# Gate sums of the next block moved into the loop over row tiles, and PSUM copies cut in halves, in an adaLN layer's forward and backward pass

## The chip, the cores and the metric

One core of a Trainium2 chip. The metric is device time in microseconds of one execution, and below it is the median of three runs.

## What is computed

One token (1 x 1024) goes through a layer with adaptive layer norm, attention over the last 4096 rows of a cache, and a gated feed-forward part. The program returns the output and the gradients of nine inputs. The part that the change touches is the feed-forward part, forward and backward:

```python
h = _layernorm(x) * (1 + cb) + sb
g = h @ w_gate            # 1024 x 3584
u = h @ w_up              # 1024 x 3584
out = x + gb * ((_sigmoid(g) * u) @ w_down)      # 3584 x 1024
# and, through jax.vjp, the gradients of w_gate, w_up, w_down and h
```

With one token every weight gradient is an outer product of two vectors and as large as its weight. The gradients of the two caches (1 x 4 x 65536 x 128 each) are zero outside the last 4096 rows, and these zeros have to be written too; the page shows 114 writes of 1024 KB from the tile of zeros, which fill the queue of transfers wherever the program puts them.

## The kernel before, in words

The program is written in one order by hand; each engine (PE, ACT, DVE, POOL for the software DMA queue, SP for the hardware one) carries out its share of it in that order, waiting on semaphores that the framework derives from the tiles. Transfers are issued by POOL (weights in, gradients out, zeros) and by SP (w_down and its gradient).

The feed-forward part runs over 7 blocks q of 512 hidden columns. For a block:

- `load_ug` (L863, DMA on POOL at L865) has brought w_up and w_gate, 1024 x 512 each, as eight row tiles j of 128 rows, rows 0 to 3 and rows 4 to 7 in separate DMAs of 512 KB. There are two buffers, `ug_v[:, q % 2]`; block q + 2 goes where block q was, so its loads wait until block q's gradients have been stored from there.
- `load_wd` on SP (L852) has brought 512 rows of w_down in two halves s. There is one buffer, `wd_v`.
- `front(q)` (L955) sums h2 x w_up and h2 x w_gate on PE in 64 narrow matmuls; `gates(q)` (L961, L962) takes sigmoids on ACT; `hh_ops(q)` makes small products on DVE.
- `ffn_mm(q, s)` (L973, PE) is the forward product with w_down. `wd_ttr(q, s)` (L979 through the helper at L210, DVE) is the row sums of w_down x upstream gradient. `wd_outer(q, s)` (L983 through L206, DVE) overwrites w_down's tile with its gradient, and `store_wd` (L855) sends it out.
- `dug_part(q)` makes the gradient of gate and up: eight transposes on PE into one PSUM tile of 128 x 1024 bf16 (tp_dug, L992), then one ACT copy that spreads it as a row over all partitions (`dug_b`, which lives in the tile scr, L993).
- The loop over the row tiles j (L1021): `ttr(w, w, dug_b, ...)` on DVE (L210) sums w x dug_b, then the tile is overwritten with an outer product h2[j] x dug_b, on ACT for j below 5 (`outer_act`, L241) and on DVE for the rest (`outer_dve`, L206). After j = 3 the rows 0 to 3 are stored (`store_ug`, L869 on POOL), after j = 7 the rest. `zero(z[..])` puts one or more writes of zeros into POOL's queue at four places per block.

Besides this there are 45 side jobs that no block needs but the work after the loop does: `tr_unit` (L833) transposes a 128 x 1024 block in place, eight PE transposes into a PSUM tile (tp_side, L837) and one ACT copy back (L838). `side(n)` runs the next n of them. They and `dug_part` take their PSUM tile from the same pool with one buffer (`new_tp`), so that they follow each other on it. In a block before the change they stand after the outer products of tiles 1 to 4 (in the first block 3 and 4), after `wd_ttr(q + 1, 0)`, after `gates(q + 1)` and at the end.

After the loop over j a block goes on with block q + 1: `wd_ttr(q+1, 0)`, `front`, `gates`, `hh_ops`, `ffn_mm` twice, `wd_outer(q+1, 0)`, `wd_ttr(q+1, 1)`, `dug_part(q+1)`, the loads of block q + 2, `wd_outer(q+1, 1)`.

Of the kernel before, what the change touches and what calls it, by code (L numbers as in the profile page):

```python
# [19 lines left out]
D = 1024  # L20
# [38 lines left out]
def kernel(  # L59
# [26 lines left out]
    nc = tc.nc  # L86
# [60 lines left out]
    def dep(later, earlier):  # L147
        tc.add_manual_dep(later.ins, earlier.ins.name,
                          mybir.DependencyInfo(mybir.DependencyClass.Sync, mybir.DependencyReason.DATA),
                          reason="pace")  # L150

    def zero(n, after=None):
        for _ in range(n):
            if len(zleft) <= keep[0]:
                return
            region, narrow_ = zleft.pop(0)
            first = None
            if narrow_:
                nc.gpsimd.inc_swdge_sem([], [], mode="reset_dge_cursor")  # L160
                n = nlen - ncount.pop()
                first = nc.gpsimd.dma_start(
                    out=rest[0:NS, 0:nlen * 128].rearrange("p (t x) -> p t x", t=2)[:, :, n * 64:(n + 1) * 64],
                    in_=zeros[0:NS, 0:64].rearrange("p (t x) -> p t x", t=1).broadcast_to([NS, 2, 64]))
                ins = nc.gpsimd.dma_start(
                    out=region[8:P, :].bitcast(FP32).rearrange("(t p) x -> p t x", t=2),
                    in_=zeros[0:60, :].rearrange("p (t x) -> p t x", t=1).broadcast_to([60, 2, ZW // 2]))
            else:
                ins = nc.gpsimd.dma_start(out=region.bitcast(FP32), in_=zeros[:, :])  # L169
            if after is not None:  # L170
                dep(first or ins, after)
# [5 lines left out]
    def next_pool():  # L177
        nrot[0] += 1
        return rot[nrot[0] % len(rot)]
# [8 lines left out]
    def new_tp(name="tp"):  # L188
        p, tag = next_pool()
        return p.tile([P, 1024], BF16, name=name, tag=tag)  # L190
# [4 lines left out]
    def mulv(out, a, b):  # L195
        return tt(out, a, b, ALU.mult)

    def addv(out, a, b):
        return tt(out, a, b, ALU.add)

    def cp(out, a):
        return nc.vector.tensor_copy(out=out, in_=a)  # L202
# [6 lines left out]
    def ttr(out, w, b, acc):  # L209
        return nc.vector.tensor_tensor_reduce(out=out, in0=w, in1=b, scale=1.0, scalar=0.0,  # L210
                                              op0=ALU.mult, op1=ALU.add, accum_out=acc)
# [31 lines left out]
    def outer_dve(out, col, b):  # L243
        return ts(out, b, col, ALU.mult)
# [200 lines left out]
    def side(n=1):  # L445
        for _ in range(n):
            if jobs:
                jobs.pop(0)()
# [61 lines left out]
    for tb in range(4):  # L510
        c = slice(tb * 1024, (tb + 1) * 1024)
        nc.scalar.activation(out=P_bf[:, c], in_=P_bf[:, c], func=ACT.Exp, bias=nbias[:, 0:1], scale=SCALE,
                             accum_out=ssum4[:, tb:tb + 1])
        tp = new_tp("tp_pT")
# [111 lines left out]
    for g in range(G):  # L626
        nbank = bank_pair("n_ps", g)
        for t_ in range(KT):
            s = g * KT + t_
# [200 lines left out]
    b_sec(3, 4, 40)  # L830
    zero(Z_CB)

    def tr_unit(blk, dst=None):  # L833
        def run():
            tp = new_tp("tp_side")
            for i in range(8):
                nc.tensor.transpose(tp[:, i * P:(i + 1) * P], blk[:, i * P:(i + 1) * P], ident_bf[:, :])  # L837
            nc.scalar.copy(out=blk if dst is None else dst, in_=tp[:, :])  # L838
        return run

    wg_view = B_w_gate.rearrange("(j p) n -> p j n", p=P)
# [9 lines left out]
    def load_wd(q, s):  # L851
        nc.sync.dma_start(out=wd_v[:, 2 * s:2 * s + 2, :], in_=wd_dram(B_w_down, q, s))  # L852

    def store_wd(q, s):
        nc.sync.dma_start(out=wd_dram(out_8, q, s), in_=wd_v[:, 2 * s:2 * s + 2, :])  # L855
# [7 lines left out]
    def load_ug(q, j0, n):  # L863
        for k, view in ((0, wu_view), (1, wg_view)):
            nc.gpsimd.dma_start(out=ug_tile(q, k, j0, n), in_=ug_part(view, q, j0, n))  # L865

    def store_ug(q, j0, n):
        for k, view in ((0, dwu_view), (1, dwg_view)):
            nc.gpsimd.dma_start(out=ug_part(view, q, j0, n), in_=ug_tile(q, k, j0, n))  # L869
# [45 lines left out]
    fold_half(6, 0)  # L915
    bch(1)
    tr_unit(B_t[6], ar(60, 2))()
    load_wd(0, 1)
    fold_half(6, 1)
# [17 lines left out]
    dug_b = scr  # L937
# [10 lines left out]
    def front(q):  # L948
        gu = gu_t[q % 2]
        for k in range(2):  # L950
            for j in range(KD):
                for i in range(4):
                    f0 = 256 * (i // 2) + i % 2
                    col = 4 - 4 * k + i
                    nc.tensor.matmul(gu[:, col:col + 1], lhsT=ug_v[:, q % 2, j // 4, j % 4, k, f0:f0 + 255:2],  # L955
                                     rhs=h2_bf[:, j:j + 1], start=(j == 0 and i == 0), stop=(j == KD - 1),
                                     skip_group_check=True)

    def gates(q):
        r, gu = small[q % 2], gu_t[q % 2]  # L960
        nc.scalar.activation(out=r["sg"], in_=gu[:, 0:4], func=ACT.Sigmoid)  # L961
        nc.scalar.activation(out=r["om"], in_=gu[:, 0:4], func=ACT.Sigmoid, scale=-1.0)  # L962

    def hh_ops(q):
        r, up = small[q % 2], gu_t[q % 2][:, 4:8]
        mulv(r["hh_bf"], r["sg"], up)
        mulv(r["hh"], r["sg"], up)
        mulv(r["hom"], r["hh"], r["om"])

    def ffn_mm(q, s):  # L970
        for i in (2 * s, 2 * s + 1):
            for k in range(KD):
                nc.tensor.matmul(ffn_ps[:, k:k + 1], lhsT=wd_v[:, i, k * P:(k + 1) * P],  # L973
                                 rhs=small[q % 2]["hh_bf"][:, i:i + 1], start=(i == 0 and k == 0),
                                 stop=(i == 3), skip_group_check=True)

    def wd_ttr(q, s):
        for i in (2 * s, 2 * s + 1):
            ttr(junk, wd_v[:, i, :], b1k, small[q % 2]["dhh"][:, i:i + 1])  # L979

    def wd_outer(q, s):
        for i in (2 * s, 2 * s + 1):
            outer_dve(wd_v[:, i, :], small[q % 2]["hh"][:, i:i + 1], b1k)  # L983
        store_wd(q, s)

    def dug_part(q):
        r = small[q % 2]
        mulv(r["dug_bf"][:, 0:4], r["dhh"], r["sg"])
        mulv(r["dug_bf"][:, 4:8], r["dhh"], r["hom"])
        tp = new_tp("tp_dug")  # L990
        for i in range(8):
            nc.tensor.transpose(tp[:, i * P:(i + 1) * P], r["dug_bf"][:, i:i + 1].broadcast_to([P, P]), ident_bf[:, :])  # L992
        nc.scalar.copy(out=dug_b.rearrange("p (s f j) -> p s f j", s=4, j=2),  # L993
                       in_=tp.rearrange("p (s j f) -> p s f j", s=4, j=2))

    jobs.append(tr_unit(B_t[7]))
    for h in range(HQ):
# [3 lines left out]
    def unpark(p):  # L1001
        nc.scalar.copy(out=B_home[p], in_=BT_ps[p][:, :])

    wd_ttr(0, 0)
    side(1)
    front(0)
# [1 line left out]
    hh_ops(0)  # L1008
    ffn_mm(0, 0)
    ffn_mm(0, 1)  # L1010
    wd_ttr(0, 1)
    dug_part(0)
    wd_outer(0, 0)
    wd_outer(0, 1)
    zero(Z_FOLD[2])
    load_wd(1, 0)
    load_wd(1, 1)
    for q in range(NB):
        z = Z_FFN[q]
        more = q + 1 < NB  # L1020
        for j in range(KD):  # L1021
            w = ug_v[:, q % 2, j // 4, j % 4, :, :].rearrange("p k f -> p (k f)")
            ttr(w, w, dug_b, dh2acc[:, q * KD + j:q * KD + j + 1])
            if not more and j in (3, 5, 6):
                unpark({3: 2, 5: 0, 6: 4}[j])
            (outer_act if j < 5 else outer_dve)(w, h2[:, j:j + 1], dug_b)
            if more and (0 if q else 2) < j < 5:
                side()
            if j == 0:
                if q == 0:  # L1030
                    cp(ffn, ffn_ps)
                else:
                    addv(ffn, ffn, ffn_ps)
            if j == 3:
                store_ug(q, 0, 4)
                zero(z[0])
        store_ug(q, 4, 4)
        zero(z[1])
        if more:
            wd_ttr(q + 1, 0)  # L1040
            side()
            front(q + 1)
            gates(q + 1)
            side()
            hh_ops(q + 1)
            ffn_mm(q + 1, 0)
            ffn_mm(q + 1, 1)
            wd_outer(q + 1, 0)
            wd_ttr(q + 1, 1)
            dug_part(q + 1)  # L1050
            if q + 2 < NB:
                load_ug(q + 2, 0, 4)
            wd_outer(q + 1, 1)
            zero(z[2])
            side(2 if q < 4 else 1)
            if q + 2 < NB:
                load_ug(q + 2, 4, 4)
            zero(z[3])
            if q + 2 < NB:
                load_wd(q + 2, 0)  # L1060
                load_wd(q + 2, 1)
        else:
            zero(z[2] + z[3])
    assert not jobs
    for p in (1, 3, 5):
        unpark(p)

# [266 lines left out]
```

## Time and profile before

| | before |
|---|---|
| median of three runs | 601.25 us (599.19 to 601.6) |
| the profiled execution's own time | 599.74 us |
| its span | 598.0 us |
| busy: PE, ACT, DVE | 409.9, 265.2, 337.7 us |
| bytes moved | 246.63 MB, 412 GB/s over the span |
| read from HBM, written to HBM | 60.30 MB, 185.60 MB |
| side transposes, L837 | 432, 52.2 us |
| side copies, L838 | 54, 54.0 us, 1012 ns each |
| copies of the gate gradient, L993 | 7, 7.1 us |
| outer products on ACT, L241 | 35, 39.4 us, 1148 ns each |

The profile is of one execution. "Busy" is the time in which an engine worked; it says nothing of which engine was waited for. A group of instructions is named by its source line, the engine, and the tiles written and read. The chain of work that ended last is followed back from the last instruction to whatever released it. The rate of the transfers in a stretch of time, in GB/s, tells how well the sixteen DMA engines were fed there.

### The profile page before, as it was taken

The numbers are of one execution on the slowest core, as the hardware profiler recorded it, in microseconds if no ns is written. First come the engines' busy times: TensorE is split into PE (matmuls) and PEld (weight loads), VectorE is DVE, ScalarE is ACT, GpSimd is POOL, SyncE is SP. The second block draws the span as 40 slices with busy tenths as digits, with TensorE's granted clock in tenths as the row PEclk, the third lists the DMA queues.
The fourth block names the chain that finished last, engine by engine and source line by source line (L and its number), as shares of the span: only waits on it lengthen the run. The fifth ranks groups of instructions, "written<-read, shape, count | busy, mean of one in ns | idle before, by whom it ended". The sixth has DMA issues, their size and how long they took to land. (4 is left out here: it accounts for less than half of the span.)

```text
span 598.0 us, 11036 instructions
## 1 busy us (share of the span) xinstructions
PE 409.9 (69%) x4586; PEld 277.9 (46%) x4612; DVE 337.7 (56%) x641; ACT 265.2 (44%) x408; POOL 157.7 (26%) x253
## 2 busy tenths in 40 slices
PE   3997688999899989989983235454445195795120
PEld 3996333334344545546663234344344174585120
DVE  3653499999511010070019387787778886878170
ACT  3479514567311014212135245746746834893110
POOL 3113123222223213222222224323343162232100
PEclk9999699999999999999995555555555576855555
DMA  8999999999999999999999999999999999999997
GB/s 352 418 418 421 412 426 402 427 423 425 427 418 427 421 427 424 420 424 425 423 395 410 421 411 399 405 399 413 406 396 413 417 423 413 420 424 424 426 425 296
DMA packets 45026, 246.63 MB, mean 412 GB/s; under 512 B 5085, under 2 KB 5085, under 8 KB 24544
## 3 DMA queue, kind: packets, MB, share of 16 engines
q0 software_dynamic: 37536, 217.60, 94.9%
q1 hardware_dynamic: 7392, 28.32, 13.3%
q8 instruction: 36, 0.59, 0.4%
q14 instruction: 14, 0.11, 0.1%
q10 hardware_dynamic: 48, 0.01, 0.0%
HBM read 60.30 MB, written 185.60 MB: 411 GB/s over the span
## 5 line engine op out<-in xcount | busy, mean ns | idle before, releaser
L692 PE MATMUL b_ps<-arena 128*128 128x512 bf16 x493 | 113.4, 379 | 1.1 <-issue 0.2
L169 POOL DMA_DIRECT2D out_dram<-zeros x114 | 62.7, 551 | 169.8 <-DMA out_dram<-zeros 46.0
L837 PE MATMUL tp_side<-ident_bf,arena 128*128 128x128 bf16 x432 | 52.2, 301 | 52.0 <-ACT arena L838 43.2
L193 DVE TENSOR_TENSOR arena<-arena 128x2048 bf16<-128x2048 bf16 x64 | 76.6, 1224 | 2.3 <-PE n_ps L637 0.3
L692 PEld LDWEIGHTS <-arena 128*128 128x128 bf16 x512 | 48.7, 98 | 55.9 <-issue 2.9
L837 PEld LDWEIGHTS <-arena 128*128 128x128 bf16 x432 | 44.1, 140 | 58.6 <-issue 58.3
L210 DVE CUSTOM_DVE_ANT_0 arena<-arena,scr 128x1024 bf16<-128x1024 bf16 x56 | 66.2, 1221 | 8.6 <-ACT scr L993 8.6
L838 ACT COPY arena<-tp_side 128x1024 bf16<-128x1024 bf16 x54 | 54.0, 1012 | 37.5 <-PE tp_side L837 36.7
L637 PE MATMUL n_ps<-arena 128*128 128x512 bf16 x249 | 65.1, 378 | 6.9 <-DVE arena L193 5.0
L210 DVE CUSTOM_DVE_ANT_0 junk<-arena,b1k 128x1024 bf16<-128x1024 bf16 x28 | 34.2, 1222 | 21.2 <-DMA arena<-in_B_w_down_dram 20.6
L637 PEld LDWEIGHTS <-arena 128*128 128x128 bf16 x256 | 24.6, 97 | 41.6 <-issue 16.2
L241 ACT ACTIVATE arena<-scr,h 128x1024 bf16<-128x1024 bf16 x35 | 39.4, 1148 | 1.4 <-DVE dh2acc L210 1.3
L869 POOL DMA_DIRECT2D out_dram<-arena x28 | 21.4, 771 | 67.7 <-ACT arena L241 61.0
L202 DVE CAST arena<-b_ps 128x512 bf16<-128x512 f32 x6 | 4.2, 692 | 61.6 <-PE b_ps L692 61.6
L1163 ACT ACTIVATE arena<-ps_kv 128x512 bf16<-128x512 f32 x48 | 26.1, 680 | 28.5 <-PE ps_kv L1159 28.3
L1159 PE MATMUL ps_kv<-junk,arena 8*128 8x128 bf16 x256 | 26.9, 303 | 16.4 <-DVE arena L206 14.9
L601 ACT CAST arena<-t_ps 128x512 bf16<-128x512 f32 x56 | 30.1, 589 | 12.1 <-PE t_ps L599 12.1
L1159 PEld LDWEIGHTS <-arena 8*128 8x128 bf16 x256 | 25.0, 140 | 18.1 <-issue 18.1
L456 ACT COPY arena<-tp_wq 128x1024 bf16<-128x1024 bf16 x23 | 21.8, 1032 | 8.3 <-PE tp_wq L454 8.3
L993 ACT COPY scr<-tp_dug 128x1024 bf16<-128x1024 bf16 x7 | 7.1, 1012 | 40.5 <-PE tp_dug L992 36.2
L206 DVE TENSOR_SCALAR arena<-arena,cs_col 128x4096 bf16<-128x4096 bf16 (+1 forms) x16 | 16.1, 1020 | 12.6 <-DMA out_dram<-arena 12.6
L878 ACT CAST arena<-fold_ps 128x512 bf16<-128x512 f32 x16 | 9.4, 587 | 28.3 <-PE fold_ps L876 28.3
(302 smaller groups left out, 645.9 us busy)
## 6 DMA issues: line engine op xcount, KB each, us to landing
out_dram<-zeros POOLq DMA_DIRECT2D x114, 1024.0 KB, 15.1
out_dram<-arena POOLq DMA_DIRECT2D x27, 1024.0 KB, 18.1
out_dram<-arena POOLq DMA_DIRECT2D x30, 512.0 KB, 8.3
out_dram<-arena SPq DMA_DIRECT2D x20, 512.0 KB, 9.5
arena<-in_A_wq_dram POOLq DMA_DIRECT2D x8, 1024.0 KB, 20.5
arena<-in_A_wo_dram POOLq DMA_DIRECT2D x8, 1024.0 KB, 11.6
arena<-in_w_mod_dram POOLq DMA_DIRECT2D x7, 1024.0 KB, 17.7
arena<-in_B_w_down_dram SPq DMA_DIRECT2D x14, 512.0 KB, 9.6
```

Source lines behind the costliest of these rows:

```text
L169: ins = nc.gpsimd.dma_start(out=region.bitcast(FP32), in_=zeros[:, :])
L193: return nc.vector.tensor_tensor(out=out, in0=a, in1=b, op=op)
L210: return nc.vector.tensor_tensor_reduce(out=out, in0=w, in1=b, scale=1.0, scalar=0.0, op0=ALU.mult, op1=ALU.add, accum_out=acc)
L241: return nc.scalar.activation(out=out, in_=b, func=ACT.Copy, scale=col)
L456: nc.scalar.copy(out=blk, in_=tp[:, :])
L601: nc.scalar.copy(out=o, in_=ps)
L637: mm = nc.tensor.matmul(nbank[k][:, :], lhsT=k_nat[:, g, t_ * DH:(t_ + 1) * DH], rhs=vp[:, t_ % 2, 4 * k:4 * k + 4, :].rearrange("p h d -> ...
L692: mm = nc.tensor.matmul(bbank[p][k][:, :], lhsT=a4[:, p, h, :], rhs=wo_t[u][:, a, k * 512:(k + 1) * 512], start=(i == 0 and a == 0), stop= ...
L837: nc.tensor.transpose(tp[:, i * P:(i + 1) * P], blk[:, i * P:(i + 1) * P], ident_bf[:, :])
L838: nc.scalar.copy(out=blk if dst is None else dst, in_=tp[:, :])
L1159: nc.tensor.matmul(ps[:, t4 * DH:(t4 + 1) * DH], lhsT=rows[32 * g:32 * g + HG, t_ * P:(t_ + 1) * P], rhs=hd[32 * g:32 * g + HG, :], start= ...
L1163: nc.scalar.activation(out=o, in_=ps[:, :], func=ACT.Copy, scale=float(scale))
```

## The change

There are four parts. One PSUM tile (`ffn_tp`) is taken once and is shared by all side jobs and by `dug_part` in this part of the program. The copies out of it are cut into two half copies of 512 columns. `front(q + 1)` and `gates(q + 1)` move into the loop over row tiles, behind the fifth outer product, and `hh_ops(q + 1)` stands ahead of `wd_ttr(q + 1, 0)`. The side jobs go to other places: none before tile 5, then one after each of tiles 5 to 7, two (in the first block three) after the loop, one after `wd_outer(q + 1, 0)` and one at the end. Ahead of the loop `wd_outer(0, 0)` stands before `wd_ttr(0, 1)`, and one side job comes before the first block.

```diff
     def tr_unit(blk, dst=None):
         def run():
-            tp = new_tp("tp_side")
+            tp = ffn_tp[0] if ffn_tp else new_tp("tp_side")
+            parts = 2 if ffn_tp else 1
             for i in range(8):
                 nc.tensor.transpose(tp[:, i * P:(i + 1) * P], blk[:, i * P:(i + 1) * P], ident_bf[:, :])
-            nc.scalar.copy(out=blk if dst is None else dst, in_=tp[:, :])
+            for k in range(parts):
+                c = slice(k * D // parts, (k + 1) * D // parts)
+                nc.scalar.copy(out=(blk if dst is None else dst)[:, c], in_=tp[:, c])
         return run
...
-        tp = new_tp("tp_dug")
+        tp = ffn_tp[0]
         for i in range(8):
             nc.tensor.transpose(tp[:, i * P:(i + 1) * P], r["dug_bf"][:, i:i + 1].broadcast_to([P, P]), ident_bf[:, :])
-        nc.scalar.copy(out=dug_b.rearrange("p (s f j) -> p s f j", s=4, j=2),
-                       in_=tp.rearrange("p (s j f) -> p s f j", s=4, j=2))
+        for k in range(2):
+            c = slice(k * 512, (k + 1) * 512)
+            nc.scalar.copy(out=dug_b[:, c].rearrange("p (s f j) -> p s f j", s=2, j=2),
+                           in_=tp[:, c].rearrange("p (s j f) -> p s f j", s=2, j=2))
...
+    ffn_tp.append(new_tp("tp_ffn"))
     wd_ttr(0, 0)
     side(1)
     front(0)
...
     ffn_mm(0, 1)
+    wd_outer(0, 0)
     wd_ttr(0, 1)
     dug_part(0)
-    wd_outer(0, 0)
     wd_outer(0, 1)
+    side(1)
...
             (outer_act if j < 5 else outer_dve)(w, h2[:, j:j + 1], dug_b)
-            if more and (0 if q else 2) < j < 5:
+            if more and j == 4:
+                front(q + 1)
+                gates(q + 1)
+            if more and j > 4:
                 side()
...
         if more:
+            side(2 if q else 3)
+            hh_ops(q + 1)
             wd_ttr(q + 1, 0)
-            side()
-            front(q + 1)
-            gates(q + 1)
-            side()
-            hh_ops(q + 1)
             ffn_mm(q + 1, 0)
             ffn_mm(q + 1, 1)
             wd_outer(q + 1, 0)
+            side()
             wd_ttr(q + 1, 1)
             dug_part(q + 1)
...
             zero(z[2])
-            side(2 if q < 4 else 1)
+            side()
...
     assert not jobs
+    ffn_tp.clear()
```

More of the change, by code (lines that the diff above doesn't have):

```diff
@@ L831 @@
     zero(Z_CB)
+    ffn_tp = []
     def tr_unit(blk, dst=None):
         def run():
-            tp = new_tp("tp_side")
+            tp = ffn_tp[0] if ffn_tp else new_tp("tp_side")
+            parts = 2 if ffn_tp else 1
             for i in range(8):
                 nc.tensor.transpose(tp[:, i * P:(i + 1) * P], blk[:, i * P:(i + 1) * P], ident_bf[:, :])
-            nc.scalar.copy(out=blk if dst is None else dst, in_=tp[:, :])
+            for k in range(parts):
+                c = slice(k * D // parts, (k + 1) * D // parts)
+                nc.scalar.copy(out=(blk if dst is None else dst)[:, c], in_=tp[:, c])
         return run
```

## The prediction

> **What bounds the kernel now.** I read the page first, its slices of the span:
>
> ```profile
> DMA  8999999999999999999999999999999999999997
> GB/s 352 418 418 421 412 426 402 427 423 425 427 418 427 421 427 424 420 424 425 423 395 410 421 411 399 405 399 413 406 396 413 417 423 413 420 424 424 426 425 296
> ```
>
> The DMA engines are busy in every slice, and the page gives 246.63 MB in 598.0 us, 412 GB/s. The change moves no byte more or less, so time can only come from the slices in which less than about 420 GB/s is moved. These are slices 21 to 31 (about 314 to 478 us), which is the loop over the blocks q of the gated part, and that is where the diff is. So I cut this loop at its block borders:
>
> ```profile
> core 0: us, PE busy (x) PEld busy (x) DVE busy (x) ACT busy (x) POOL busy (x), PEclk, DMA share, GB/s
> ...
> 155.00:316.00 161.00, 151.44 (x1314) 85.14 (x1330) 29.74 (x74) 36.59 (x57) 40.86 (x68) 0.99 1.13 421
> ...
> 320.00:344.90 24.90, 6.16 (x112) 5.51 (x111) 14.37 (x30) 10.82 (x12) 5.52 (x8) 0.50 1.15 413
> 344.90:368.30 23.40, 11.26 (x158) 10.00 (x159) 17.79 (x37) 13.45 (x15) 8.31 (x13) 0.50 1.12 403
> ...
> 414.70:437.90 23.20, 11.49 (x173) 10.22 (x171) 18.07 (x37) 14.46 (x16) 8.43 (x13) 0.50 1.09 404
> ...
> 459.90:480.00 20.10, 4.19 (x56) 3.61 (x57) 16.72 (x41) 12.80 (x14) 5.14 (x8) 0.50 1.18 418
> ```
>
> The last column is the rate. It is 413 and 418 in the first and the last block and 403, 408, 407, 404, 402 in the five between. No engine is full (DVE 18 of 23 us), so a chain across engines must set their length. The chain of work that ended last shows it; from one block's gate transposes (tp_dug, L992) to the next:
>
> ```profile
> 372.30 1.05 PE tp_dug L992 x8
> 373.41 1.02 ACT scr L993
> 374.48 1.02 PE tp_side L837 x8
> 375.52 1.02 ACT arena L838
> ...
> 389.03 1.69 PE fg L955 x64
> 390.72 0.88 PE tp_side L837 x8
> 391.59 0.20 PE fg L973 x8
> 391.82 0.88 DVE arena L206 x2
> ...
> 395.37 1.05 PE tp_dug L992 x8
> ```
>
> PE fills the one PSUM tile with eight transposes, ACT empties it, PE fills it again: eight such side units to a block, at about 2.1 us each where nothing hides them. The blocks start their tp_dug at 318.96, 349.01, 372.30, 395.37, 418.58, 441.79 and 463.87. POOL's timeline shows what this does to the transfers:
>
> ```profile
> 385.08 1.50 POOL L869 DMA_DIRECT2D out_dram<-arena  x2 [9.08 <-ACT arena L241]
> ...
> 387.20 1.50 POOL L869 DMA_DIRECT2D out_dram<-arena  x2
> ```
>
> The first stores of block 2 (rows 0 to 3, called S0 here) go out 12.8 us after its tp_dug, since ACT has put a side copy between its outer products; POOL idled 9.08 us for it. In windows of 1 us the rate then is 360, 373, 385 GB/s at 387 to 390, and again 381, 324, 385 at 394 to 397, before the loads that wait for the stores to land.
>
> **What the Trainium skill says.** "Trainium Kernel Development and Optimization", Key Constraints: DMAs of SP, ACT and POOL run on the same 16 engines and interleave; the trace agrees (share above 1 with both queues active), so SP's 1 MB each way per block is in the same sum. "DMA: Bandwidth & Descriptors", Where 436 GB/s comes from: a ceiling of 435 GB/s; the trace's full stretches give 413 to 427, and I take 418, the last block's, as the rate reachable with this mix. "PSUM — Partial Sum Buffer", PSUM bank collisions raise a hardware error: PE writing and ACT reading one bank at once collide even at other columns. The trace of before never shows both on this tile. "ScalarE: Activation LUTs", What ACT_TABLE_LOAD costs: 186 ns + 0.833 ns per element, neighbours overlapping by 93 ns; 1024 elements make 1039, the trace has 1012; 512 make 613, the trace has 587 for L878 (f32 in).
>
> **The change part by part.**
>
> *Two half copies.* In the changed program only the first of a unit's eight transposes waits, for the count after both halves of the copy before, and the first half copy waits for all eight. So nothing overlaps. A pair costs 2 x 0.587 less 0.09, 1.08 us against 1.01: +0.07 a unit (bounds 0 and +0.17, no overlap).
>
> *Order in a block.* From tp_dug = 0: transposes end 1.05, the pair of dug copies 2.19 (1.11 + 1.08), one side unit (1.02 + 1.08, gaps 0.1) 4.38. DVE starts its row tiles at 2.24. ACT's five outer products, no longer cut by side copies, follow at 4.3 every 1.07 us: the fourth ends at 8.6, the fifth at 9.7. Hence S0 goes at 8.6 instead of 12.8. DVE's eight tiles take 10.89 us (374.46 to 385.35), as before, so the stores of rows 4 to 7 (S1) go at 13.1 instead of 14.9. The issue order on POOL and SP is unchanged.
>
> *Gate sums earlier.* front(q+1), 1.9 us of PE (L955), was on the chain at 1.68; now PE reaches it at 3.3, beside ACT's outer products. Gates (0.25 us, L961 and L962) at 9.8. Queued behind them on ACT: the side copies; behind the sums on PE: those units' transposes.
>
> *Rest of the block.* The first side unit's transposes are done early, its copies end at 10.9; three more at 1.02 + 1.08 + 0.08 = 2.18 end at 17.4; the fifth unit's transposes end at 18.5, and ffn_mm behind them lets DVE's wd_outer start at 18.7 (+0.23 as at 391.59 to 391.82). Then 0.88 + 2.45 (392.70 to 395.15) + 0.22: next tp_dug at 22.25. The sixth unit, its copies ending at 21.8, just fits. So compute needs 22.25 us, against 23.29, 23.07, 23.21, 23.21 in four blocks (8 units then, 7 now) and 22.08 in the fifth (7 and 7). With pairs at 1.17 it is 22.9 (7 copies in a row); with full overlap in the halves about 19, DVE's wd chain then being last.
>
> *What is late next: the DMA itself.* Window times rate gives 9.43, 9.51, 9.40, 9.37 and 8.84 MB; at 418 GB/s 22.56, 22.74, 22.49, 22.42 and 21.16 us. The larger of this and 22.25 in each block sums to 112.46 against 115.0 for 344.9 to 459.9: 2.5 us saved. The wd loads landed at tp_dug + 15.8 (388.06); DVE wants them at 13.5 now, and has until 16.3 before wd_outer at 18.7 is delayed: hidden, but if S0 pushes them back 3 us, 0.5 us a block is lost.
>
> *First block.* wd_outer(0, 0) now stands ahead of wd_ttr(0, 1): tp_dug comes 1.4 us later, S0 1.6 later, but the first wd store 2 earlier. Eight side units instead of four: the last transposes end near 341, when the wd loads land (341.50, 346.26), so they are hidden; without that cover 2.2 each. I take 0.3 us lost, bounds 1.5 lost and 1.0 gained.
>
> *Sum.* 2.5 - 0.3 = 2.2 us. The profiled execution's 599.74 us (598.0 span, 1.74 around it) becomes 597.5. It lies 1.5 under the median of the three runs, 601.25, to which the forecast is put: **599.0 us**. After the loop the rate is 419 to 428; nothing more is to be gained there.
>
> **Rivals.**
>
> *A: the transfers close up fully* (28%). All gaps to 418 go, in the first block too: 3.6 + 0.3, and if the mix carries 421, 320 to 480 gives 160 x (1 - 407.8 / 421) = 5.0 us. For it: stores leave 4 us earlier, so POOL has work ready before the queue drains. Against it: the loads still wait for the stores to land. Time: 601.25 - 4.5 = 596.8.
>
> *B: the gate sums wait for the weights: slower* (14%). front(q+1) moves from tp_dug + 16.7 into the tile loop, but its last gate weights landed at tp_dug + 11.1, 12.6, 10.7, 10.3 and 10.2 (issue 397.96 + 8.1 for the third, for instance). In the new order anything after about 8.2 delays the chain: gates, five side units and ffn_mm queue behind. These loads wait for S1 to land. S1 at 13.1, + its landing s + 1.7 for issue + load landing l, less a block T, must be under 8.2; beyond, 2T = 22.25 - 8.2 + 13.1 + 1.7 + s + l. With 8.7 and 8.9, as now, T = 23.2, no gain; with 10.1 and 10.7 (the most seen outside the first block) T = 24.8, +1.6 in four blocks and +2.7 in the fifth, some 9 us less a better filled first block: about 607. It begins to cost at s + l = 15.7 and makes the kernel slower from 17.6. For milder latencies: S1 no longer follows S0 by 2 but by 4.5 us, so less is queued ahead of it. I therefore expect s + l nearer 16.
>
> *C: the copies overlap after all, or nothing changes* (8%). With 19 us of compute the DMA still ends last: case A. Where the gap between the store waves costs what the earlier S0 brings: 601.
>
> **Numbers.** The main case has 50%, its own range 597.2 to 602.0 (pairs at 1.17 and the first block's loss at one end, at the other 1 us gained there). The range 595.3 to 604.5 takes in A and the mild half of B. About 0.5%, 3.0 us, is what a measurement can tell from no change. Faster by more: A's 28% and about 14% from the main case, 42%. Slower: 12%, from B. Within: 46%.
>
> **What would show it.** Right: tp_dug to tp_dug 22.3 to 22.8 us in blocks 1 to 5; S0 at about 8.6 and S1 at 13 after it; rates of 410 to 418 there; side transposes that never run beside their tile's copies; gates near 9.8. Wrong: PE idle before front with a DMA of the gate weights as releaser (B); blocks of 23 us with the same two dips in the rate; pairs of half copies far from 1.08; DVE waiting for w_down past 16.3; or a first block longer than 30 us.

## The result, and the profile after

The changed kernel takes 602.49 us (median of 20 runs, 600.9 to 603.59), the kernel before 600.07 us in the runs made beside it: a ratio of 1.0042, 95% interval 1.0032 to 1.0051. The forecast was 599.0 us, 0.4% faster; the time went up by 0.4%. It is still inside the stated range of 595.3 to 604.5 us: what failed is the direction. The profiled execution took 601.92 us with a span of 600.0.

The page of the changed kernel, the slices of the span:

```profile
DMA  8999999999999999999999999999999999999996
GB/s 353 418 418 421 414 426 416 427 425 426 427 419 426 423 429 421 424 424 423 421 400 415 417 402 414 401 371 408 400 388 419 409 419 402 417 423 424 427 424 283
```

The bytes are the same. Ahead of the loop over the blocks the rates are as before (418 GB/s against 417 up to 316 us), behind it they are a little lower (419 against 423 from 500 to 580 us), and in the loop two slices fall to 371 and 388, where before none was under 395. Cut at the starts of the gate transposes (the borders at 420.00 and 442.00 only roughly), with the rate as the last column:

```profile
core 0: us, PE busy (x) PEld busy (x) DVE busy (x) ACT busy (x) POOL busy (x), PEclk, DMA share, GB/s
...
318.90:347.40 28.50, 12.15 (x169) 10.34 (x169) 17.91 (x38) 15.10 (x25) 6.33 (x10) 0.50 1.11 414
347.40:373.40 26.00, 11.35 (x163) 9.70 (x164) 18.15 (x39) 14.02 (x23) 9.70 (x14) 0.50 1.09 409
373.40:398.10 24.70, 10.97 (x161) 9.33 (x159) 17.65 (x38) 14.03 (x23) 7.49 (x11) 0.50 1.05 393
398.10:420.00 21.90, 11.00 (x160) 9.51 (x160) 17.55 (x35) 13.39 (x23) 7.00 (x11) 0.50 1.12 393
420.00:442.00 22.00, 11.14 (x160) 9.59 (x160) 17.50 (x38) 13.90 (x24) 8.14 (x12) 0.50 1.13 404
442.00:466.70 24.70, 11.15 (x160) 9.60 (x160) 18.57 (x39) 14.44 (x24) 8.34 (x13) 0.50 1.07 403
```

The transposes of dug_part (L997 now) start at 318.86, 347.39, 373.21, 398.09, 420.56, 443.06 and 467.03 us. The first block is 1.5 us shorter than before, but it is no gain: counted from the first `wd_ttr`, the second block's transposes come after 36.07 us in both profiles. (That first `wd_ttr` starts at 311.3 to 315.5 us in the profiles of this document, though no run changed anything ahead of it; so lengths are compared here, not times of the clock.) The five blocks after it take 25.82, 24.88, 22.47, 22.50 and 23.97 us, 119.6 together against 114.9. Two of the five have the length that was forecast, three do not. The chain of work that ended last says why, for the block from 373.21 on:

```profile
373.72 9.65 DMA arena<-in_B_w_gate_dram
...
383.42 1.33 PE fg L960 x44
384.75 0.89 PE tp_ffn L840 x8
...
385.67 1.08 ACT arena L843 x2
...
393.31 1.01 PE tp_ffn L840 x8
394.32 0.63 PE fg L978 x24
394.95 0.48 DVE arena L206
```

The chain of before held no load of gate weights. Now it goes from that load's issue to the gate sums (L960), which start their last 44 matmuls when it lands, 10.2 us after tp_dug, and from there through the side units to ffn_mm and wd_outer. PE stops four times in these sums:

```profile
377.77 0.27 PE L960 MATMUL fg<-h_bf,arena 128*128 128x1 bf16 x4 [1.31 <-DMA arena<-in_B_w_up_dram]
...
380.33 0.48 PE L960 MATMUL fg<-h_bf,arena 128*128 128x1 bf16 x12 [2.29 <-DMA arena<-in_B_w_gate_dram]
...
382.08 0.27 PE L960 MATMUL fg<-h_bf,arena 128*128 128x1 bf16 x4 [1.27 <-DMA arena<-in_B_w_up_dram]
...
383.42 1.33 PE L960 MATMUL fg<-h_bf,arena 128*128 128x1 bf16 x44 [1.08 <-DMA arena<-in_B_w_gate_dram]
```

The program sums all of w_up (32 matmuls) before w_gate (32). So 12 of the last 44 read only w_up's rows 5 to 7, 16 more read the first half of w_gate, and all of them stand until the last load of w_gate has landed. No run tests what releasing them earlier is worth; from 1.33 us for the 44, an estimate is 0.8 us in a delayed block. The waits from 318 to 483 us (total, times, longest) name the same:

```profile
DVE arena L206 <- PE fg L978: 18.3, 6, 5.0
...
PE fg L960 <- DMA arena<-in_B_w_gate_dram: 16.5, 10, 2.3
...
PE fg L960 <- DMA arena<-in_B_w_up_dram: 13.3, 9, 2.3
```

The first row is wd_outer on DVE waiting for ffn_mm, which stands on PE behind the held-up side units. The same row of before, where no row of L955 waits for a load:

```profile
DVE arena L206 <- PE fg L973: 2.2, 6, 0.4
```

And on POOL the stores and loads have moved apart:

```profile
382.02 1.50 POOL L874 DMA_DIRECT2D out_dram<-arena  x2 [6.99 <-ACT arena L241]
383.52 0.56 POOL L169 DMA_DIRECT2D out_dram<-zeros  x1
386.87 1.50 POOL L874 DMA_DIRECT2D out_dram<-arena  x2 [2.80 <-ACT arena L843]
390.13 0.76 POOL L870 DMA_DIRECT2D arena<-in_B_w_up_dram  x1 [1.77 <-DMA out_dram<-arena]
392.80 0.75 POOL L870 DMA_DIRECT2D arena<-in_B_w_gate_dram  x1 [1.91 <-DMA out_dram<-arena]
396.39 0.75 POOL L870 DMA_DIRECT2D arena<-in_B_w_up_dram  x1 [2.84 <-issue]
397.72 0.75 POOL L870 DMA_DIRECT2D arena<-in_B_w_gate_dram  x1 [0.58 <-DMA out_dram<-arena]
```

The stores of rows 0 to 3 leave 8.8 us after tp_dug, as forecast, those of rows 4 to 7 13.7. But the second pair of loads (396.39) has to wait for the second stores, which landed 9.3 us after their issue, and meanwhile the rate falls. The stretch of 8 us around this, in the changed kernel and in the one before:

```profile
394.00:402.00 8.00, 4.54 (x73) 3.89 (x71) 6.15 (x14) 3.84 (x8) 2.79 (x4) 0.50 0.99 335
...
394.00:402.00 8.00, 3.29 (x27) 2.80 (x28) 6.62 (x14) 3.32 (x4) 2.60 (x4) 0.50 1.01 393
```

No other 8 us between 10 and 590 us are as low in either profile; the lowest of before have 377.

### The profile page after: what moved, and what is told of

It is laid out like the page before. It is cut to its first block, busy times and chain, and to the rows that moved or that the text cites. A ratio compares the mean times of both kernels' runs of the same rounds, so it can differ in the third digit from the quotient of the medians.

```text
span 600.0 us, 11090 instructions
## 1 busy us (share of the span) xinstructions
PE 411.0 (68%) x4586; PEld 277.3 (46%) x4612; DVE 337.1 (56%) x641; ACT 267.9 (45%) x460; POOL 159.4 (27%) x253
## 4 chain that ended last, share of the span: by engine, by line
PE 36%; DMA 34%; DVE 16%; ACT 6%; issue 5%; POOL 0%; DVEq 0%; ACTq 0%; POOLq 0%; SPq 0%
DMA arena<-in_B_w_gate_dram 12%; DMA out_dram<-arena 10%; PE b_ps L692 10%; DMA out_dram<-zeros 9%; PE n_ps L637 6%; DVE arena L206 5%; DVE arena L193 4%; PE tp_ffn L840 3%; ACT arena L843 2%; PE t_ps L599 2%; DVE arena L210 2%; PE tp_wq L454 2%; PE w_ps L395 1%; DMA arena<-in_B_w_down_dram 1%; PE tp_k L435 1%
## 5 line engine op out<-in xcount | busy, mean ns | idle before, releaser
L692 PEld LDWEIGHTS <-arena 128*128 128x128 bf16 x512 | 48.7, 98 | 55.8 <-issue 2.9
L840 PE MATMUL tp_ffn<-ident_bf,arena 128*128 128x128 bf16 x360 | 45.6, 308 | 41.0 <-ACT arena L843 31.8
L843 ACT COPY arena<-tp_ffn 128x512 bf16<-128x512 bf16 x90 | 48.3, 589 | 47.7 <-PE tp_ffn L840 47.7
L840 PEld LDWEIGHTS <-arena 128*128 128x128 bf16 x432 | 43.7, 139 | 46.9 <-issue 46.7
L637 PEld LDWEIGHTS <-arena 128*128 128x128 bf16 x256 | 24.6, 97 | 41.6 <-issue 16.2
L1170 PE MATMUL ps_kv<-junk,arena 8*128 8x128 bf16 x256 | 26.9, 303 | 17.0 <-DVE arena L206 15.5
L241 ACT ACTIVATE arena<-scr,h 128x1024 bf16<-128x1024 bf16 x35 | 37.3, 1148 | 0.0
L960 PE MATMUL fg<-h_bf,arena 128*128 128x1 bf16 x448 | 15.9, 166 | 31.0 <-DMA arena<-in_B_w_gate_dram 16.5
L960 PEld LDWEIGHTS <-arena 128*128 128x128 bf16 x448 | 14.4, 105 | 33.7 <-DMA arena<-in_B_w_gate_dram 17.6
L206 DVE TENSOR_SCALAR arena<-arena,cs_col 128x4096 bf16<-128x4096 bf16 (+1 forms) x16 | 16.0, 1017 | 13.2 <-DMA out_dram<-arena 13.1
## 6 DMA issues: line engine op xcount, KB each, us to landing
arena<-in_A_wo_dram POOLq DMA_DIRECT2D x8, 1024.0 KB, 12.6
```

The costliest lines, as they stand in the source:

```text
L206: return nc.vector.tensor_scalar(out=out, in0=a, scalar1=s1, scalar2=None, op0=op0)
L241: return nc.scalar.activation(out=out, in_=b, func=ACT.Copy, scale=col)
L637: mm = nc.tensor.matmul(nbank[k][:, :], lhsT=k_nat[:, g, t_ * DH:(t_ + 1) * DH], rhs=vp[:, t_ % 2, 4 * k:4 * k + 4, :].rearrange("p h d -> ...
L692: mm = nc.tensor.matmul(bbank[p][k][:, :], lhsT=a4[:, p, h, :], rhs=wo_t[u][:, a, k * 512:(k + 1) * 512], start=(i == 0 and a == 0), stop= ...
L843: nc.scalar.copy(out=(blk if dst is None else dst)[:, c], in_=tp[:, c])
L1170: nc.tensor.matmul(ps[:, t4 * DH:(t4 + 1) * DH], lhsT=rows[32 * g:32 * g + HG, t_ * P:(t_ + 1) * P], rhs=hd[32 * g:32 * g + HG, :], start= ...
```

## Theory and rivals

Theory: the gate sums, moved into the tile loop, reach PE before their weights have landed, and everything queued behind them on PE and ACT is held up. Rival one: the half copies cost the time (each pair more than one whole copy, 7 on the chain of a block). Rival two: the gap in the transfers between a block's two pairs of loads costs it, and the wait is a symptom. A third possibility, the order of the other steps, is tested along with them. All ratios below are to the kernel before, with 95% intervals; blocks are counted from the tp_dug that starts them, 0 to 5.

## Experiments

**Gate sums from weights that are already there** (`e1_resident`).

```diff
+                    w = ug_v[:, 0, j // 4, j % 4, k, f0:f0 + 255:2]
+                    if q:
+                        w = ar(128, 16)[:, (2 * j + k) * FB + f0:(2 * j + k) * FB + f0 + 255:2]
-                    nc.tensor.matmul(gu[:, col:col + 1], lhsT=ug_v[:, q % 2, j // 4, j % 4, k, f0:f0 + 255:2],
+                    nc.tensor.matmul(gu[:, col:col + 1], lhsT=w,
```

> The changed kernel, but the gate sums of blocks 1 to 6 are made from other weights that have long been in the arena, so the gate values are not the right ones; every instruction, transfer and place in the order stays. Only the wait of front(q+1) for the loads of block q+1 is gone. Theory (the sums, moved into the tile loop, wait there for the gate weights and hold up PE's side transposes, ACT's copies and ffn_mm behind them): all of blocks 1 to 5 take 22.5 us from tp_dug to tp_dug, as the two undelayed ones of the changed kernel do (22.47 and 22.50), instead of 25.8, 24.9, 22.5, 22.5, 24.0; about 7 us less than the changed kernel as far as the transfers keep up, so ratio to before 0.990 to 0.997. Rival (half copies and the new order of the side jobs cost the time): blocks keep their lengths, ratio 1.003 to 1.005.

Measured: 0.9991 (0.9982 to 1.0000). Blocks 1 to 5 take 23.01, 22.43, 22.00, 22.00 and 22.02 us, 8.2 less together than in the changed kernel, and the first 2.6 less. So the wait is what lengthened the blocks. But of 10.8 us in the loop only about 3 reach the end. The windows of this kernel, with the rate as the last column again, show where the rest went:

```profile
345.18:368.19 23.01, 10.68 (x161) 9.35 (x161) 18.12 (x39) 13.79 (x23) 8.50 (x13) 0.50 1.12 413
368.19:390.62 22.43, 10.68 (x161) 9.35 (x161) 18.05 (x39) 13.79 (x23) 6.65 (x10) 0.50 1.13 405
390.62:412.62 22.00, 10.65 (x161) 9.35 (x161) 17.97 (x39) 13.79 (x23) 7.68 (x11) 0.50 1.05 390
412.62:434.62 22.00, 10.65 (x160) 9.35 (x161) 18.22 (x39) 13.79 (x23) 8.44 (x12) 0.50 1.08 399
```

Even with blocks of 22.0 to 22.4 us the rate in the last three rows is 390 to 405, not the 418 of the forecast: something other than compute limits the transfers in this loop, and what they have not moved in it they move after it.

**Whole copies in the changed kernel** (`e2_whole`), and **half copies in the kernel before** (`e4_before_halves`). The cut is that of the first; the second is the reverse, put into the kernel before.

```diff
-            parts = 2 if ffn_tp else 1
+            parts = 1
...
-        for k in range(2):
-            c = slice(k * 512, (k + 1) * 512)
-            nc.scalar.copy(out=dug_b[:, c].rearrange("p (s f j) -> p s f j", s=2, j=2),
-                           in_=tp[:, c].rearrange("p (s j f) -> p s f j", s=2, j=2))
+        nc.scalar.copy(out=dug_b.rearrange("p (s f j) -> p s f j", s=4, j=2),
+                       in_=tp.rearrange("p (s j f) -> p s f j", s=4, j=2))
```

> The changed kernel with one copy of 1024 columns in place of each pair of half copies; the rest as changed. Theory: the waits for the gate weights stay, only the 7 copies on the chain of a block get 0.06 us shorter each, so blocks shorten by 0.4 us at most where compute sets them; ratio to before 1.001 to 1.004. Rival (the half copies are what made it slower): back to before or under it, 0.996 to 1.000.

> The kernel before with nothing but the half copies (side jobs and the gate gradient's row), each unit with its own tile from the pool. Theory: no overlap, each pair 1.07 instead of 1.01 us, five to eight on a block's chain: 0.3 to 0.6 us a block, ratio 1.001 to 1.005. Rival (halves let PE write one half while ACT reads the other): under 0.998. If all of the change's loss is in the halves, the ratio is 1.004 here too.

Measured: 1.0029 (1.0020 to 1.0039) for the first, 1.0016 (1.0005 to 1.0027) for the second. A pair of half copies takes 1.07 us in the trace, a whole copy 1.01. In the kernel before the halves lengthen blocks 2 and 3 from 23.07 and 23.21 to 23.73 and 23.62. In neither trace does a half copy run beside transposes into the same tile. So they cost some 0.1 to 0.2%, but they are not the main part: without them the changed kernel is still slower.

**Gate sums behind the tile loop** (`e3_front_after_tiles`).

```diff
-            if more and j == 4:
-                front(q + 1)
-                gates(q + 1)
...
+            front(q + 1)
+            gates(q + 1)
             side(2 if q else 3)
```

> The changed kernel with front(q+1) and gates(q+1) put behind the tile loop, after the three side jobs of tiles 5 to 7; half copies, the one tile and the other places as changed. Theory: PE has three units' transposes to do before it reaches the sums at about tp_dug + 14, when the gate weights have landed (by + 11.1), so the wait is gone; the sums come back on the chain with 1.7 us less what they hide, blocks of 22.8 to 23.4 us, ratio 0.996 to 1.000. Rival (something else of the change): ratio stays at 1.003 to 1.005.

Measured: 1.0005 (0.9994 to 1.0016). The loss is gone with this one part taken back, and the other parts together, which no run takes apart, cost no more than 0.16%. The length of the blocks was not as expected throughout: 24.39, 25.72, 22.26, 22.87 and 23.36 us, 118.6 together against 119.6 in the changed kernel. Most of what is gained is in the first block (24.97 against 28.53). In blocks 1 and 2 PE still waits 2 to 3 us for the weights, even at this later place.

**Zeros between the two pairs of loads, in the changed kernel** (`e8_after_zeros`) **and in the kernel before** (`e7_before_zeros`). POOL's queue gets one of a block's writes of zeros between load_ug(q+2, 0, 4) and load_ug(q+2, 4, 4) instead of behind both.

```diff
-Z_FFN = [(1, 1, 0, 2), (1, 1, 0, 1)] + [(1, 0, 0, 2)] * 3 + [(1, 1, 1, 2), (1, 2, 1, 0)]
+Z_FFN = [(1, 1, 1, 1), (1, 1, 1, 0)] + [(1, 0, 1, 1)] * 3 + [(1, 1, 1, 2), (1, 2, 1, 0)]
```

> The changed kernel with nothing but the zeros moved between the two groups of loads. Theory: the gap is filled but the gate weights of rows 4 to 7 land up to 2.5 us later and front in the tile loop waits that much longer: blocks of 25 to 28 us, ratio 1.004 to 1.012. Rival (the gap in the transfers, not the wait for the weights, is what made the changed kernel slower): back to 1.000 or under.

> The kernel before with nothing but one megabyte of zeros per block moved between the two groups of loads (blocks 0 to 4). Theory: its second dip (324 to 385 GB/s at 394 to 397 us), some 0.4 us a block, is filled, and the first dip, ahead of the stores, gets deeper by as much, since fewer zeros are left behind the loads: 0.998 to 1.002. Rival (that gap is worth a lot by itself): under 0.997.

Measured: 1.0115 (1.0093 to 1.0138) in the changed kernel, 0.9984 (0.9973 to 0.9995) in the one before. This separates the theory from rival two: the same filling takes 0.16% off the kernel before and adds 0.73% to the changed one, which had 1.0042, because the loads it stands in front of are the ones that the gate sums wait for. PE's and DVE's timeline of block 1, whose tp_dug is at 348.58:

```profile
363.18 1.33 PE L960 MATMUL fg<-h_bf,arena 128*128 128x1 bf16 x44 [2.33 <-DMA arena<-in_B_w_gate_dram]
...
364.82 0.16 DVE L193 TENSOR_TENSOR hh_bf<-sg,fg 128x4 bf16<-128x4 f32 x1 [3.12 <-ACT om L967]
```

The weights land at + 14.6, and the block takes 29.28 us; with compute at 22.5 and 8.2 as the point from which lateness counts, it would be 22.5 + 6.4 = 28.9. In the four blocks after it the last 44 sums start at + 9.1, + 8.1, + 10.2 and + 8.2, which gives 23.4, 22.5, 24.5 and 22.5 in the same way; they take 23.79, 22.77, 24.91 and 22.84. The chain that ended last goes through the load of gate weights in each of these five blocks.

**Zeros between the loads, with gate sums from resident weights** (`e5_resident_zeros`; the two edits above together).

> As the run with gate sums from resident weights (wrong gate values in blocks 1 to 6), and besides one megabyte of zeros per block is issued between the loads of rows 0 to 3 and those of rows 4 to 7 of block q+2 instead of behind both (blocks 0 to 4); the bytes are the same. Theory of the second bound (when compute no longer holds it up, the loop is bound by the round of store, landing, load, landing on POOL, with a gap in the transfers while POOL waits for the stores of rows 4 to 7 to land): the gap is filled, the rate from 350 to 460 us rises from about 400 to 410 or more, ratio to before 0.992 to 0.997. Rival (the transfers are as full as this mix allows): 0.998 to 1.000 as without the zeros moved.

Measured: 0.9958 (0.9944 to 0.9973). The mean rate from 316 to 500 us goes from 408 to 413 GB/s. So the gap is real and worth about 2 us, once no wait for the weights hides it.

**A version of the parts that help** (`e6_combined`): the gate sums behind the tile loop, whole copies, zeros between the loads; the one PSUM tile, the places of hh_ops, of the side jobs and of wd_outer(0, 0) as in the changed kernel.

> A version with right results: the changed kernel with the gate sums behind the tile loop, whole copies, and one megabyte of zeros per block moved between the two groups of loads. Theory: no wait for gate weights before tp_dug + 14, 0.4 us a block less in copies, the gap between the loads filled; the loads of rows 4 to 7 land about 2.5 us later, up to + 13.5, still in time. Blocks of 22.5 to 23 us, ratio 0.993 to 0.998. If the zeros only push the loads back: 1.000 to 1.004.

Measured: 0.9979 (0.9967 to 0.9991), faster than both kernels. Its blocks 1 to 5, in the same columns:

```profile
345.87:371.70 25.83, 10.81 (x161) 9.51 (x161) 18.30 (x39) 13.42 (x15) 10.17 (x15) 0.50 1.17 414
371.70:397.48 25.78, 10.81 (x160) 9.51 (x161) 17.82 (x39) 13.42 (x15) 7.85 (x11) 0.50 1.09 402
397.48:419.63 22.15, 10.51 (x161) 9.37 (x161) 18.01 (x39) 13.42 (x15) 7.46 (x11) 0.50 1.08 410
419.63:441.58 21.95, 10.57 (x160) 9.43 (x161) 18.02 (x39) 13.41 (x15) 8.12 (x12) 0.50 1.10 413
441.58:463.54 21.96, 10.50 (x161) 9.36 (x161) 17.82 (x39) 13.42 (x15) 7.76 (x12) 0.50 1.13 414
```

Three blocks have 22 us at 410 to 414 GB/s. Blocks 1 and 2 are long, since PE waits there for weights (1.3 to 2.2 us at a time), probably because their loads stand behind the first block's backlog; at 414 GB/s block 1 loses no transfers by it.

**Three variants of it**: zeros moved in blocks 2 to 4 only (`e9_late_zeros`), wd_ttr(q+1, 0) ahead of hh_ops(q+1) again (`e11_ttr_first`), and the sums behind all side jobs (`e10_front_last`).

```diff
+            side(2 if q else 3)
             front(q + 1)
             gates(q + 1)
-            side(2 if q else 3)
             hh_ops(q + 1)
             wd_ttr(q + 1, 0)
```

> The combined version, with the zeros moved between the loads in blocks 2 to 4 only and left behind them in blocks 0 and 1. In the combined run the gate weights still came last in the blocks after tp_dug 1 and 2 (25.83 and 25.78 us), where a backlog fills the queue anyway. Theory: these loads land up to 2.5 us earlier, the two blocks shorten by 1 to 2 us each; since the transfers are full there, little of it reaches the end: ratio 0.996 to 0.999. If the zeros are needed there too: 0.999 to 1.001.

> The combined version, with wd_ttr(q+1, 0) ahead of hh_ops(q+1) again, as in the kernel before. In the run with the sums last, DVE stood 6.7 us a block at hh_ops waiting for the gates with the 2.4 us of wd_ttr(q+1, 0) queued behind. Theory: where gates come late (the blocks after tp_dug 1 and 2 of the combined version, 25.83 and 25.78 us) the row sums now run in the wait, and these two blocks shorten by up to 2.4 us each; the others, at 22 us, stay. With the transfers full at 412 GB/s in the loop only part of it reaches the end: ratio 0.994 to 0.998. If DVE then stands at wd_ttr for w_down instead, so that nothing is gained: 0.997 to 0.999.

> The combined version, with the gate sums and gates behind all five side jobs (six in the first block), right ahead of hh_ops. Theory: PE reaches the sums at about tp_dug + 18, after every load has landed, so no block waits for weights, but the sums and gates stand on the chain with about 2 us: blocks of 23.5 to 24.5 us, all alike, where the combined version has 22.0 or 25.8. Ratio 0.998 to 1.003, not faster than the combined version.

Measured: 0.9978 (0.9968 to 0.9988), 0.9976 (0.9964 to 0.9987) and 1.0243 (1.0225 to 1.0262). The first two cannot be told from the combined version. In the first of them block 1 became short and block 2 longer (22.59 and 26.55 us), and blocks 4 and 5 went from 22 to 23.68 and 23.82; in the second blocks 1 and 2 stayed at 25.76 and 25.69. The last was far outside what I expected. Its blocks are alike, at 26.0 us (376.51 to 402.54, for instance), not 23.5 to 24.5; the timeline shows what was left out of the sum:

```profile
395.97 0.17 ACT L966 ACTIVATE sg<-fg 128x4 f32<-128x4 f32 x1 [0.67 <-PE fg L960]
...
396.24 0.16 DVE L193 TENSOR_TENSOR hh_bf<-sg,fg 128x4 bf16<-128x4 f32 x1 [6.68 <-ACT om L967]
...
396.61 0.99 PE L978 MATMUL fg<-hh_bf,arena 128*128 128x1 bf16 x32 [0.68 <-DVE hh L193]
```

DVE stands 6.68 us at hh_ops for the gates, with the 2.4 us of wd_ttr(q+1, 0) behind it in its queue, where the changed order has put them. So late gates cost in two places; this is read from the timeline, no run separates it here. Blocks 1 to 5 take 130.4 us against 114.9, +15.5, and the whole kernel +15: these longer blocks cost in full. The shorter blocks of `e1_resident` gave back about a third against the changed kernel, and the changed kernel's own +4.8 us cost 2.4. So the length of the blocks alone does not give the time.

The rate does. The bytes are fixed, so lost time is rate not had; this tells where time was lost, not why. From 316 to 500 us the mean rate was 409 GB/s before, 405 changed, 413 combined, 397 in `e8_after_zeros` and 374 in `e10_front_last`; from 500 to 580 it was 423, 419, 422, 419 and 419. For the changed kernel 184 x 4 / 409 + 80 x 4 / 423 = 2.6 us, measured 2.4; for `e8_after_zeros` 5.4 + 0.8 = 6.2, measured 6.8; for `e10_front_last` 15.7 + 0.8 = 16.5, measured 15.1; for the combined one -1.8 + 0.2 = -1.6, measured -1.5. For `e1_resident` (408, 423) it gives +0.4 where -0.5 was measured, and in the seven other runs it is off by 0.4 to 0.8 us: one profiled execution, with the rate rounded to 1 GB/s, does not settle less than a microsecond.

## Why the prediction was wrong, step by step

- **Half copies**: right. Nothing overlaps in the trace, a pair is 1.07 us (1.08 said).
- **Order in a block**: right. Stores at 8.8 and 13.7 us after tp_dug (8.6 and 13.1 said), five outer products in 5.31.
- **Compute of a block**: right where it sets the length: 22.47 and 22.50, and 22.00 with resident weights, against 22.25.
- **First block**: right within its bounds. From the first wd_ttr to tp_dug 7.5 us instead of 6.0, so the 1.4 us of delay was right; the block itself is 1.5 us shorter, so that nothing is lost, where 0.3 us was said. But it hides a wait that was not foreseen: with resident weights the 36.07 us to the second tp_dug are 33.15.
- **Gate sums earlier**: this step failed. Its sum put front at 3.3 us after tp_dug and the gates at 9.8, "beside ACT's outer products", as if the weights were there: it put the wait for them at nothing. Rival B had the mechanism, the place and the threshold of 8.2 us, and it was given 14% on the ground "I therefore expect s + l nearer 16". Measured, block by block from the first on, the landing s of the second stores (with POOL's own delay in it) and the landing l of the last gate weights were 14.7 + 10.0, 11.4 + 9.7, 9.5 + 6.6, 8.0 + 7.3 and 9.2 + 7.9. The expectation holds for the weights that blocks 3 and 4 wait for (16.1 and 15.3) and nearly for block 5's (17.1). In blocks 1 to 5 the weights landed at + 11.1, + 10.2, + 6.2, + 7.7 and + 9.3; what exceeds 8.2, added to 22.5, gives 25.4, 24.5, 22.5, 22.5 and 23.6, and the blocks took 25.82, 24.88, 22.47, 22.50 and 23.97. I had excluded the first block's latencies as special; but block 1 waits for the loads that follow the first block's stores, with the sums now early enough to feel it. In the kernel before these weights landed no earlier (10.2 to 12.6 us after tp_dug, as rival B lists), and nothing waited, because the sums came at 16.7.
- **"What is late next: the DMA itself"**: the second failure. It took the larger of compute and bytes / 418 as a block's length. Without the wait compute was 22.0 us and the loop still moved only 390 to 405 GB/s in blocks 2 to 4. Moving the first stores 4 us earlier did not take away the dip beside them (1 us windows of 360, 373 and 385 GB/s at 387 to 390 before, 373, 287 and 348 at 383 to 386 now), and it made the second one longer (381, 324 and 385 at 394 to 397 before; now all of 394 to 402 is under 370), where POOL waits for the second stores and the zeros stand behind the loads that wait. I had this as a part of rival C, at 601, within its 8%; it belonged into the main case. The 2.5 us of gain were never to be had from the order of the compute alone: with the wait gone the kernel is 0.1% faster, and only with the zeros moved as well 0.4%.

Shown, then: the wait for the gate weights makes the blocks long (`e1_resident`, `e8_after_zeros`), and moving the sums back takes the loss away (`e3_front_after_tiles`). Also shown: the half copies cost 0.16% in the kernel before. How the changed kernel's 0.42% divides between the two stays open to about 0.1%: `e2_whole` takes 0.13% off, but its interval overlaps the changed kernel's own.

## What to carry to other kernels

When work is moved ahead in an in-order queue, look up when its operands land, block by block and not in a steady block alone, and list what then queues behind it; here a step of 1.9 us moved off the chain brought a 10 us transfer onto it. In a kernel bound by transfers ask of every edit what it does to the rate: here compute made shorter gave back a third in one run, compute made longer cost in full in another. A filler in the queue belongs in front of the instruction that will block the queue, unless somebody waits for what is behind it: the same move took 0.16% off one order and added 0.73% to the other.

## What the runs showed of the hardware that was not expected

The landing time of a 512 KB transfer in the loop was anything from 5.7 us (stores at 385.08 before) to 15.0 (stores at 332 before), with 401 and 417 GB/s moved meanwhile, so its size does not tell it; what was queued ahead of it is the likely reason, which no run separates. Two half copies of 128 x 512 from PSUM take 589 ns each and 1.07 us together, so the second starts about 0.1 us before the first ends.
